# Window attention ahead of two feed-forward nets on one core: another layout for the global keys, their products by array quarters, and the attention outputs copied at another place

## The chip, the core and the metric

One NeuronCore of a Trainium2 chip runs the whole program. The metric is the device time of one execution in microseconds (us). The kernel before took 911.26 us (median of three runs, 911.12 to 912.29). In the text PE is TensorE, DVE is VectorE, ACT is ScalarE, POOL is GpSimd and SP is SyncE, as in the profile.

## The reference, cut to what matters

```python
# q_l, k_l, v_l: [4, 8, 512, 64]; q_g, k_g, v_g: [4, 8, 32, 64]
s_g   = scale * q_g @ concat(k_g, k_l)^T            # 32 global queries see all 544 keys
out_g = softmax(s_g) @ concat(v_g, v_l)
s_ll  = where(|i - j| <= 32, scale * q_l @ k_l^T, -1e9)   # local queries: a window ...
s_l   = concat(scale * q_l @ k_g^T, s_ll)                 # ... and the 32 global keys
out_l = softmax(s_l) @ concat(v_g, v_l)
x = concat(out_g, out_l)        # as [2176 tokens, 512]
h = x @ w_in;  x = (h * cos(h)) @ w_out              # first net, 512 -> 2048 -> 512
h = max(x @ w_in2, 0);  out = (h * h) @ w_out2       # second net, the same sizes
```

The four weight matrices come as float64. The chip makes float32 of their bits and splits each number into a high and a low part, so that a matrix product is three products of the parts.

## The kernel before, in words

**Items and steps.** The attention is cut into 40 items. For each batch and each pair of heads (there are 16 pairs, `p`) there are two `Local` items, each for 256 queries; behind each two pairs comes one `Global` item, so the items repeat as four Local and one Global. A loop over steps `s` runs them as a pipeline. In each step the list `CFG["order"]` gives the order in which parts are issued, and `CFG["lag"]` says of which item: the scores (`S`) of item s, the maxima and exponentials (`SM`) of item s, the reciprocals and the scaling (`RC`, `NM`) of item s-1, the transposes of the weights (`TM`) of item s-2, their evacuation (`TE`) of item s-3, the output products (`OM`) and the copy of the outputs (`OE`) of item s-4. Each engine works strictly in the order of issue, so the list also sets each engine's own order.

**A Local item.** `kT[p]` holds K^T of a pair of heads in eight blocks of 160 columns: 64 keys, the next 64 keys (a copy of the next block, made by POOL in `k_copy`), and the 32 global keys (also copied by POOL). The scores are eight products of a quarter of the PE array each (64 rows by 64 columns of it): rows by head, columns by half of the queries. DVE adds the mask and takes the maximum of each of four units, ACT makes the exponentials, POOL and DVE scale them, PE transposes them (`tw` for the window's part, `tg` for the global keys' part of all four units together), ACT brings them to SBUF, and `o_mm` multiplies by V. There the global keys' part is done with all 128 rows of the array: `VGZ` holds V of the global keys with zeros in the rows of the other units, and the product for each block of queries and each head uses one half of the array's columns. The outputs of an item go to one PSUM bank (6 and 7 by turns), and DVE copies them to `xt` with one instruction of 256 columns.

**Conversion of the weights.** `Feed` turns 64 pieces of the weights (a "job": 128 by 512 numbers) from float64 to float32 through five stages, one stage a step: a load, nothing, `conv_a` (POOL and ACT), `conv_b` (two DVE instructions, `CB` in the list), `conv_c` (POOL). `begin(rate)` starts a job when the credit is full. `split` makes the high part (two ACT instructions, L228) and on its next call the low part (one POOL and one DVE instruction, L214). Within the attention steps jobs start by a rate, `split` is called at the steps in `CFG["split"]`, and `CFG["sx"]` names the steps in which the first inputs of the nets are split (L744, L745).

**The nets.** From step 40 on `ffn_step` issues the products of the first net in between; 160 such steps follow, each with 12 products of 436 (or 512, 384) columns for `h` and 12 for `y`.

**PSUM banks.** Banks 0 and 1 take all transposes by turns, 2 the transposed global part, 3 to 5 the scores (two banks for an item, by turns), 6 and 7 the outputs.

The lines that the prediction touches: the scores L420, the maxima L436, the reciprocals L460 and L463, the scaling L475 (DVE for the first unit, POOL for three), the K copies L351, L353 and L361, the transposes L488 and L489, the output products L504 (global keys) and L516 (window), the copies of the outputs L529 and L633, the conversion L143, L146, L154, L155, L165, and the splits L228 and L214.

Of the kernel before, what the change touches and what calls it, by code (L numbers as in the profile page):

```python
# [19 lines left out]
P = 128  # L20
# [6 lines left out]
           'RC', 'NM', 'CB', 'LV', 'OE', 'TRQ', 'QE', 'KC', 'TM'],  # L27
# [19 lines left out]
 'free': -5,  # L47
 'kb': 'P',
 'split': [22, 24, 27, 29, 33],
 'sx': [32, 34, 37, 39],  # L50
 'arate': 0.5,
 'rate': 0.5,
 's0': 5,
# [6 lines left out]
RATE, ARATE, XD, NRING = CFG["rate"], CFG["arate"], CFG["xd"], CFG["nr"]  # L60

@with_exitstack
def kernel(
# [191 lines left out]

    KTB = 2 * 64 + SG
    masks = [ep.tile([P, 160], F32, name=f"mask{i}") for i in range(3)]
# [56 lines left out]
    def load_vg(b):  # L314
        for u in range(4):
            nc.sync.dma_start(
                VGZ[b % 2][32 * u : 32 * u + 32, :, u, :],
                v_g[b].rearrange("(k h) p d -> p k h d", h=2)[:, :, u // 2, :],
            )

    def tr_k(p):
        b, kk = divmod(p, NPAIR)
        tk = bank(BT, "tk")
        for c in range(4):
            nc.tensor.transpose(  # L325
                tk[:, c * P : (c + 1) * P],
                kn[p // 2][:, c, 2 * (p % 2) : 2 * (p % 2) + 2].rearrange("p h d -> p (h d)"),
                ident,
            )
        t = ep.tile([P, 8, KTB], F32, tag="kT", name="kT", bufs=3)  # L330
        kT[p] = t
        tks[p] = tk

    def k_evac(p):
        t, tk = kT[p], tks.pop(p)
        nc.scalar.activation(
            t[:, :, 0:64], tk.rearrange("p (j q) -> p j q", q=64), AF.Copy
        )
        if CFG["kb"] == "A":
            nc.scalar.activation(  # L340
                t[:, :, 128:KTB], tk[:, 0:SG].unsqueeze(1).to_broadcast([P, 8, SG]), AF.Copy
            )
        elif CFG["kb"] == "D":
            nc.vector.tensor_copy(
                t[:, :, 128:KTB], tk[:, 0:SG].unsqueeze(1).to_broadcast([P, 8, SG])
            )

    def k_copy(p):
        t = kT[p]
        one = dict(scalar1=1.0, scalar2=1.0, op0=ALU.mult, op1=ALU.mult)  # L350
        nc.gpsimd.tensor_scalar(t[:, 0:7, 64:128], t[:, 1:8, 0:64], **one)  # L351
        if CFG["kb"] == "P":
            nc.gpsimd.tensor_scalar(  # L353
                t[:, :, 128:KTB], t[:, 0, 0:SG].unsqueeze(1).to_broadcast([P, 8, SG]), **one
            )
        if p > 1:
            k_tail(p)

    def k_tail(p):
        b, kk = divmod(p, NPAIR)  # L360
        nc.gpsimd.tensor_scalar(  # L361
            kT[p][:, 7, 64:128], ktail[:, kk, b, :], 1.0, 1.0, op0=ALU.mult, op1=ALU.mult
        )
# [41 lines left out]

    class Local:
# [19 lines left out]

        def softmax(self):
            self.pt = lp.tile([P, 4, KTB], F32, tag="pt", name="pt", bufs=4)  # L430
            self.st = lp.tile([P, 3, 4], F32, tag="st", name="st", bufs=4)

            def unit(u):
                i = 2 * self.hb + u % 2
                m = masks[1] if i == 0 else masks[2] if i == 3 else masks[0]
                nc.vector.tensor_tensor_reduce(  # L436
                    out=self.pt[:, u, :],
                    in0=self.s[u // 2][:, 160 * (u % 2) : 160 * (u % 2) + 160],
                    in1=m,
                    scale=-0.125,  # L440
                    scalar=3.0e38,
                    op0=ALU.add,
                    op1=ALU.min,
                    accum_out=self.st[:, 0, u : u + 1],
                )
# [9 lines left out]
            return [lambda u=u: unit(u) for u in range(4)]  # L455
# [10 lines left out]
        def norm(self):  # L466
# [3 lines left out]
                self.pt[:, :, P:KTB],  # L470
                self.st[:, 2, :].unsqueeze(2).to_broadcast([P, 4, SG]),
                op=ALU.mult,
            )
            for u in range(4):
                (nc.vector if u < CFG["ndv"] else nc.gpsimd).tensor_scalar(  # L475
                    self.pt[:, u, 0:P],
                    self.pt[:, u, 0:P],
                    self.st[:, 2, u : u + 1],
                    1.0,
                    op0=ALU.mult,  # L480
                    op1=ALU.mult,
                )

        def t_mm(self):
            self.tw = bank(BT, "tw").rearrange("p (u q) -> p u q", u=4)
            self.tg = bank(BG, "tg")[:, 0:P]
            for u in range(4):
                nc.tensor.transpose(self.tw[:, u, :], self.pt[:, u, 0:P], ident)  # L488
# [11 lines left out]
        def o_mm(self):  # L500
            self.o = bank(BO, "o")[:, 0:256].rearrange("p (i q) -> p i q", i=2)
            for i in range(2):
                for h in range(2):
                    nc.tensor.matmul(  # L504
                        self.o[64 * h : 64 * h + 64, i, :],
                        lhsT=VGZ[self.b % 2][:, self.kk, 2 * h + i, :],
                        rhs=self.tgs,
# [3 lines left out]
                    )  # L511
                for half in range(2):
                    v = (VB if half else VA)[self.p // 2 % 2]
                    q = slice(64 * half, 64 * half + 64)
                    for h in range(2):
                        nc.tensor.matmul(  # L516
                            self.o[64 * h : 64 * h + 64, i, q],
                            lhsT=v[:, 2 * self.hb + i, 2 * (self.p % 2) + h, :],
                            rhs=self.tws[:, 2 * h + i, q],
# [5 lines left out]
        def o_evac(self):  # L525
            c0 = self.b * SL + 256 * self.hb
            dst, src = xt[:, self.kk, c0 : c0 + 256], self.o.rearrange("p i q -> p (i q)")
            if CFG["oe"][self.hb] == "D":
                nc.vector.tensor_copy(dst, src)  # L529
            else:  # L530
                nc.scalar.activation(dst, src, AF.Copy)


    class Global:
# [3 lines left out]
        def s_mm(self):  # L538
            self.s = []
            for n in (320, 256):  # L540
                s = bank(BT if CFG["sgb"] >> (n == 256) & 1 else BS, "sg")
                self.s.append(s)
                for i in range(2):
# [5 lines left out]
                        rhs=t[:, 0:5, 0:64] if n == 320 else t[:, 5:8:2, 0:128],  # L549
# [64 lines left out]
        def o_mm(self):  # L614
            self.o = bank(BO, "og")[:, 0 : 2 * SG].rearrange("p (i q) -> p i q", i=2)
# [33 lines left out]
    for h in range(2):  # L649
# [6 lines left out]
            out=masks[0][s, 64:128], in_=masks[0][s, 64:128], pattern=[[-1, 64]],  # L656
# [5 lines left out]
    nc.vector.memset(masks[2][64:128, 96:128], NEG)  # L662
# [361 lines left out]
```

## Time and profile before

| | |
|---|---|
| median of the runs | 911.26 us |
| the profiled execution's own time | 911.74 us |
| its span, first to last instruction | 910.0 us |
| busy PE / DVE / ACT / POOL | 890.7 / 502.5 / 439.4 / 447.8 us |
| products of the nets (L757 and L786), busy | about 403 us for h and 568 us for y, overlapping |
| attention steps 0 to 39, first scores to the first product of a net | 9.05 to 146.06 us |

The table's first lines say how long the program takes, the middle one how busy each engine was. A busy PE of 98% says little of its rate, since matmuls overlap; what tells is where PE stood still, and for that one looks at stretches. In a timeline the first number is the start, the second the time to the end of the last instruction of the row; the distance of two starts is what the engine needed, since neighbours overlap. Where a row ends in a bracket, the engine stood idle before it, and the bracket names who ended the wait. A group that works in its engine's own time and waits for nothing has no bracket; an instruction that sits on its engine until a semaphore comes can also show as a long duration.

### The profile page before, as it was taken

The page shows a single profiled execution, that of the slowest core. Times are in us where ns is not written, and L with a number is a line of the kernel's source. Part 1 is how long each engine was busy: PE and PEld are TensorE (multiplying, and loading weights), DVE is VectorE, ACT ScalarE, POOL GpSimd, SP SyncE. Part 2 cuts the span into 40 slices and gives each one's busy share as a digit, 9 for nine tenths or more (in the row PEclk, how much of TensorE's full clock was granted, in tenths as well). Part 3 has the DMA queues.
Part 4 walks back from the last instruction along what each step waited for, and adds up shares of the span by engine and source line. Part 5 has one row for each costly group of instructions (what it writes and reads, how often), then busy time and mean ns, then how long its engine had stood idle before and what let it go on. Part 6 is the DMA issues. An engine that isn't in the chain of part 4 may idle for free.

```text
span 910.0 us, 15436 instructions
## 1 busy us (share of the span) xinstructions
PE 890.7 (98%) x5720; PEld 793.7 (87%) x5720; DVE 502.5 (55%) x1058; ACT 439.4 (48%) x1036; POOL 447.8 (49%) x517
## 2 busy tenths in 40 slices
PE   7899999999999999999999999999999999999997
PEld 5777777999999999999999988889999888899996
DVE  5687899866776666765554483433422833232221
ACT  5778787665655545545444553333334632222211
POOL 4577888754574435744342484444423842222221
PEclk9999999999999999999999999999999999999999
DMA  7888643221122111121110021111100101010001
GB/s 168 192 192 195 165 129 94 71 70 53 49 62 70 47 53 61 50 70 47 47 47 1 1 70 47 53 44 66 47 1 1 47 1 47 1 47 1 35 35 36
DMA packets 82075, 57.10 MB, mean 63 GB/s; under 512 B 58320, under 2 KB 74704, under 8 KB 82000
## 3 DMA queue, kind: packets, MB, share of 16 engines
q1 hardware_dynamic: 79824, 55.59, 22.0%
q8 instruction: 45, 0.74, 0.3%
q10 hardware_dynamic: 2176, 0.52, 0.3%
q14 instruction: 30, 0.25, 0.1%
HBM read 47.45 MB, written 4.46 MB: 57 GB/s over the span
## 4 chain that ended last, share of the span: by engine, by line
PE 91%; DVE 3%; DMA 2%; ACT 1%; SPq 1%; POOL 1%; issue 1%; ACTq 0%; POOLq 0%; DVEq 0%
PE h L757 41%; PE y L786 41%; PE s L420 2%; PE tw L488 1%; PE o L504 1%; PE tq L368 1%; DVE pt L436 1%; PE o L516 1%; PE og L622 1%; DMA raw<-in_moe_w_out_dram 1%; PE sg L546 1%; PE tk L325 0%; ACT pt L446 0%; SPq L292 0%; PE twg L603 0%
## 5 line engine op out<-in xcount | busy, mean ns | idle before, releaser
L757 PE MATMUL h<-x,w 128*128 128x436 f32 (+3 forms) x1920 | 403.4, 358 | 0.0
L857 POOL TENSOR_TENSOR glo<-cr,ghi 128x436 fp32r<-128x436 f32 (+3 forms) x160 | 186.8, 1167 | 407.7 <-ACT ghi L851 393.9
L757 PEld LDWEIGHTS h<-x,w 128*128 128x128 f32 x1920 | 354.6, 188 | 27.5
L786 PE MATMUL y<-ghi,w 128*128 128x436 f32 (+1 forms) x640 | 177.6, 358 | 0.0
L846 DVE TENSOR_TENSOR cr<-h,cr 128x436 f32<-128x436 f32 (+3 forms) x160 | 96.6, 605 | 134.0 <-ACT cr L837 115.0
L786 PE MATMUL y<-w,ghi 128*128 128x512 f32 x544 | 168.4, 390 | 0.0
L745 DVE TENSOR_TENSOR x<-xt,x 128x436 fp32r<-128x436 f32 (+3 forms) x100 | 102.5, 1035 | 93.3 <-ACT x L744 78.3
L837 ACT ACTIVATE cr<-h 128x384 f32<-128x384 f32 (+1 forms) x80 | 42.8, 535 | 210.7 <-PE h L757 209.4
L786 PEld LDWEIGHTS y<-ghi,w 128*128 128x128 f32 x640 | 120.3, 188 | 6.1
L786 PEld LDWEIGHTS y<-w,ghi 128*128 128x128 f32 x544 | 101.4, 188 | 18.9
L786 PE MATMUL y<-glo,w 128*128 128x436 f32 (+1 forms) x320 | 114.8, 359 | 0.0
L786 PE MATMUL y<-w,glo 128*128 128x512 f32 x272 | 106.8, 393 | 0.0
L851 ACT ACTIVATE ghi<-cr 128x436 fp32r<-128x436 f32 (+3 forms) x160 | 89.7, 560 | 24.5 <-DVE cr L846 23.6
L831 ACT ACTIVATE ck<-h 128x436 int32<-128x436 f32 (+1 forms) x80 | 42.6, 532 | 113.1 <-PE h L757 113.1
L833 DVE SCALAR_TENSOR_TENSOR cr<-h,ck 128x436 f32<-128x436 f32 (+1 forms) x80 | 48.6, 607 | 84.9 <-ACT ck L831 84.9
L165 POOL TENSOR_TENSOR r<-cu,cc 128x512 uint32<-128x512 uint32 x64 | 85.0, 1328 | 2.0 <-DVE cc L155 2.0
L744 ACT ACTIVATE x<-xt 128x436 fp32r<-128x436 f32 (+3 forms) x100 | 55.1, 560 | 20.2 <-PE h L757 19.9
L786 PEld LDWEIGHTS y<-glo,w 128*128 128x128 f32 x320 | 60.1, 188 | 2.7
L786 PEld LDWEIGHTS y<-w,glo 128*128 128x128 f32 x272 | 51.0, 188 | 10.8
L842 ACT ACTIVATE cr<-cr,halfpi 128x436 f32<-128x436 f32 (+1 forms) x80 | 52.5, 657 | 10.1 <-DVE cr L833 10.1
L155 DVE SCALAR_TENSOR_TENSOR cc<-raw,cc 128x512 uint32<-128x512 uint32 x64 | 55.7, 870 | 0.0
L446 ACT ACTIVATE pt<-pt,st 128x160 f32<-128x160 f32 x128 | 53.3, 425 | 4.1 <-DVE st L436 4.1
(91 smaller groups left out, 907.4 us busy)
## 6 DMA issues: line engine op xcount, KB each, us to landing
raw<-in_moe_w_in_dram SPq DMA_DIRECT2D x32, 512.0 KB, 3.7
raw<-in_moe_w_out_dram SPq DMA_DIRECT2D x32, 512.0 KB, 3.5
vb<-va SPq DMA_DIRECT2D x16, 256.0 KB, 4.6
out_dram<-ypart SPq DMA_DIRECT2D x16, 256.0 KB, 2.1
qn<-in_q_l_dram SPq DMA_DIRECT2D x28, 128.0 KB, 3.7
va<-in_v_l_dram SPq DMA_DIRECT2D x24, 128.0 KB, 3.3
kn<-in_k_l_dram SPq DMA_DIRECT2D x21, 128.0 KB, 3.0
va<-in_v_l_dram SPq DMA_DIRECT2D x8, 96.0 KB, 3.2
```

The source lines that it names most:

```text
L155: lambda: v.scalar_tensor_tensor(c, t[:, :, 1].bitcast(U32), 0x80000000, c, op0=ALU.bitwise_and, op1=ALU.bitwise_or,),
L165: nc.gpsimd.tensor_tensor(ring[g][:, q, :].bitcast(U32), u, c, op=ALU.add)
L446: nc.scalar.activation(self.pt[:, u, :], self.pt[:, u, :], AF.Exp, bias=self.st[:, 0, u : u + 1], scale=-1.0, accum_out=self.st[:, 1, u : ...
L744: nc.scalar.activation(hi, xr, AF.Copy)
L745: return lambda: (nc.vector if kk in XD else nc.gpsimd).tensor_tensor(lo, xr, hi.bitcast(F32), op=ALU.subtract)
L757: nc.tensor.matmul(h, lhsT=w[:, ws, 0, kk * P : (kk + 1) * P], rhs=x, start=(k == 0), stop=(k == 3 * NK - 1),)
L786: nc.tensor.matmul(o, lhsT=l, rhs=r, start=(c_first and k == 0), stop=(c_last and k == 2))
L833: lambda: nc.vector.scalar_tensor_tensor(r, h, INV2PI, k, op0=ALU.mult, op1=ALU.subtract),
L842: nc.scalar.activation(ctmp[s], ctmp[s], AF.Sin, bias=halfpi, scale=TWOPI)
L846: nc.vector.tensor_tensor(r, hps.pop(s), r, op=ALU.mult)
L851: nc.scalar.activation(ghi[s], ctmp[s], AF.Copy)
L857: nc.gpsimd.tensor_tensor(lo, ctmp.pop(s), hi.bitcast(F32), op=ALU.subtract)
```

## The change

Five things are changed together.

1. **K^T's layout.** `kT[p]` is now nine blocks of 96 columns: 64 keys and then the 32 global keys. The 160 columns that a score product reads are the keys of a block, the global keys and the keys of the next block, in one run. POOL's copy of the next block (L351) is gone; the copy of the global keys (eight times) and of the tail remain. The masks move accordingly, and the scaled weights go to a new tile `pn`, since the window's two parts are now apart in `pt`.
2. **The global keys' output products by quarters.** The units are renumbered (u = 2 * block + head), so that the transposed global part holds a block of queries in each half of its rows. Each product takes 64 rows and 64 columns of the array, and the two blocks' outputs go to two banks. `out_half` gives each item a pair of 128-column pieces, one in bank 6 and one in bank 7, by turns left and right.
3. **The copy of the outputs** is two instructions of 128 columns, and `OE` stands right behind `SM` in the list, ahead of `RC`, `NM` and `CB`.
4. **The conversion** starts jobs at 13 named steps, and `split` is called at 21, 26, 31, 36 and 39.
5. In the nets' steps the rate of new jobs is 0.55 instead of 0.5.

```diff
-           'RC', 'NM', 'CB', 'LV', 'OE', 'TRQ', 'QE', 'KC', 'TM'],
+           'OE', 'RC', 'NM', 'CB', 'LV', 'TRQ', 'QE', 'KC', 'TM'],
- 'split': [22, 24, 27, 29, 33],
+ 'split': [21, 26, 31, 36, 39],
- 'arate': 0.5,
- 'rate': 0.5,
- 's0': 5,
+ 'begin': [9, 11, 14, 16, 19, 21, 24, 26, 29, 31, 34, 36, 39],
+ 'rate': 0.55,
...
+    obank = [ps.tile([P, 512], F32, tag=f"bank{k}", name="o") for k in BO]
+    def out_half():
+        k = turn["o"] = turn.get("o", 1) ^ 1
+        return [t[:, P * k : P * k + P] for t in obank]
...
-        t = ep.tile([P, 8, KTB], F32, tag="kT", name="kT", bufs=3)
+        t = ep.tile([P, 9, 64 + SG], F32, tag="kT", name="kT", bufs=3)
...
-        nc.gpsimd.tensor_scalar(t[:, 0:7, 64:128], t[:, 1:8, 0:64], **one)
...
+        nc.gpsimd.tensor_scalar(
+            t[:, 0:8, GK], t[:, 0, 0:SG].unsqueeze(1).to_broadcast([P, 8, SG]), **one
+        )
...
-                            rhs=kT[self.p][d, j, :],
+                            rhs=kT[self.p].rearrange("p j q -> p (j q)")[d, 96 * j : 96 * j + KTB],
...
-            self.pt = lp.tile([P, 4, KTB], F32, tag="pt", name="pt", bufs=4)
+            self.pt = lp.tile([P, 5, KTB], F32, tag="pt", name="pt", bufs=3)
...
-                    self.pt[:, u, 0:P],
-                    self.pt[:, u, 0:P],
+                    self.pn[:, u].rearrange("p (a q) -> p a q", a=2),
+                    windows(self.pt, u),
...
-            self.o = bank(BO, "o")[:, 0:256].rearrange("p (i q) -> p i q", i=2)
+            self.o = out_half()
             for i in range(2):
+                r = slice(64 * i, 64 * i + 64)
                 for h in range(2):
                     nc.tensor.matmul(
-                        self.o[64 * h : 64 * h + 64, i, :],
-                        lhsT=VGZ[self.b % 2][:, self.kk, 2 * h + i, :],
-                        rhs=self.tgs,
+                        self.o[i][64 * h : 64 * h + 64],
+                        lhsT=VGZ[self.b % 2][r, self.kk, 2 * i + h, :],
+                        rhs=self.tgs[r],
...
-            dst, src = xt[:, self.kk, c0 : c0 + 256], self.o.rearrange("p i q -> p (i q)")
...
+            for i in range(2):
+                nc.vector.tensor_copy(xt[:, self.kk, c0 + P * i : c0 + P * i + P], self.o[i])
...
-                cb = feed.begin(ARATE if due(CFG["free"]) is None else 0.0) if s >= CFG["s0"] else []
+                cb = feed.begin(1.0 if s in CFG["begin"] else 0.0)
```

PE's instructions of step 7 (the scores of item 7, then the output products of the Local item 3, then transposes), with the semaphores that a row waits for. Before:

```order
L420 MATMUL s<-kT,qT 64x160
L420 MATMUL s<-kT,qT 64x160 [waits DVE_49,PE_49]
L420 MATMUL s<-kT,qT 64x160 x6
L504 MATMUL o<-tgs,vgz_89 64x128 x2
L516 MATMUL o<-tws,va_85 64x64 x2
L516 MATMUL o<-tws,vb_87 64x64 x2
L504 MATMUL o<-tgs,vgz_89 64x128 x2
L516 MATMUL o<-tws,va_85 64x64 x2
L516 MATMUL o<-tws,vb_87 64x64 x2
```

The same place in the changed kernel:

```order
L423 MATMUL s<-kT,qT 64x160
L423 MATMUL s<-kT,qT 64x160 [waits DVE_49,PE_49]
L423 MATMUL s<-kT,qT 64x160 x6
L509 MATMUL o<-tgs,vgz_91 64x128 [waits DVE_49]
L509 MATMUL o<-tgs,vgz_91 64x128
L509 MATMUL o<-tgs,vgz_91 64x128 [waits DVE_49]
L509 MATMUL o<-tgs,vgz_91 64x128
L522 MATMUL o<-tws,va_87 64x64 x2
L522 MATMUL o<-tws,vb_89 64x64 x2
L522 MATMUL o<-tws,va_87 64x64 x2
L522 MATMUL o<-tws,vb_89 64x64 x2
```

The four products with the global keys now stand together, and the first for each bank waits for DVE. That wait is for the copies of the item just before: both items use the same two banks, in different columns.

DVE's instructions at the end of step 21 (the last maximum of item 21, then what follows it). Before:

```order
L436 ISA pt,st<-s,mask_84 128x160
L436 ISA st 128x1
L460 TENSOR_SCALAR st<-st 128x4
L463 RECIPROCAL st<-st 128x4
L475 TENSOR_SCALAR pt<-pt,st 128x128
L154 TENSOR_SCALAR cu<-cu 128x512
L155 SCALAR_TENSOR_TENSOR cc<-raw,cc 128x512
L529 COPY xt<-o 128x256
```

The same place in the changed kernel:

```order
L439 ISA pt,st<-s,mask_86 128x160
L439 ISA st 128x1
L534 COPY xt<-o 128x128 x2
L463 TENSOR_SCALAR st<-st 128x4
L466 RECIPROCAL st<-st 128x4
L479 TENSOR_SCALAR pn<-pt,st 128x128
```

The copy, now two, has moved ahead of the reciprocals; the conversion of this step (cu, cc) now stands one step later.

ACT's instructions from the exponentials of step 21 on (`tws`, `tls` and `tgs` are evacuations of transposes, `w` the high part of a weight tile). Before:

```order
L446 ACTIVATE pt,st<-pt,st 128x160 x4
L611 ACTIVATE tws<-twg 128x512
L612 ACTIVATE tls<-tlg 32x128
L336 ACTIVATE kT<-tk 128x8x64
L446 ACTIVATE pt,st<-pt,st 128x160 x4
L228 ACTIVATE w<-r 128x512 x2
L494 ACTIVATE tws<-tw 128x512
L498 ACTIVATE tgs<-tg 128x128
```

The same place in the changed kernel:

```order
L449 ACTIVATE pt,st<-pt,st 128x160 x4
L226 ACTIVATE w<-r 128x512 x2
L614 ACTIVATE tws<-twg 128x512
L615 ACTIVATE tls<-tlg 32x128
L343 ACTIVATE kT<-tk 128x8x64
L449 ACTIVATE pt,st<-pt,st 128x160 x4
L498 ACTIVATE tws<-tw 128x512
L502 ACTIVATE tgs<-tg 128x128
```

The two copies of the weight tile have moved one step forward, from behind the exponentials of step 22 to behind those of step 21.

## Rows read from the trace of the kernel before

**Rows 1.** Windows: stretch, its length, each engine's busy us (instructions), PE's clock, DMA.

```profile
59.50:75.17 15.67, 15.67 (x255) 12.75 (x254) 13.08 (x63) 12.62 (x50) 13.06 (x27) 1.00 0.92 200
75.17:93.41 18.24, 17.39 (x255) 13.75 (x254) 13.84 (x64) 14.25 (x53) 12.15 (x27) 0.91 0.80 188
...
126.42:146.30 19.88, 17.23 (x268) 13.04 (x268) 19.14 (x76) 16.47 (x60) 17.28 (x30) 1.00 0.36 108
...
161.40:900.00 738.60, 738.60 (x3628) 673.97 (x3627) 372.93 (x536) 319.76 (x609) 331.65 (x288) 1.00 0.13 41
```

**Rows 2.** Timeline of PE, step 17: start, us, line, shapes, records.

```profile
65.64 0.77 PE L420 MATMUL s<-kT,qT 64*64 64x160 f32 x16
66.35 0.44 PE L504 MATMUL o<-tgs,vgz 128*64 128x128 f32 x4
66.62 0.28 PE L516 MATMUL o<-tws,va 128*64 128x64 f32 x4
...
66.85 0.39 PE L504 MATMUL o<-tgs,vgz 128*64 128x128 f32 x4
67.07 0.28 PE L516 MATMUL o<-tws,va 128*64 128x64 f32 x4
67.18 0.29 PE L516 MATMUL o<-tws,vb 128*64 128x64 f32 x4
67.40 0.66 PE L325 MATMUL tk<-ident,kn 128*128 128x128 f32 x4
```

**Rows 3.** Timeline of PE, step 19, output products behind a Global item's scores.

```profile
73.03 0.39 PE L504 MATMUL o<-tgs,vgz 128*64 128x128 f32 x4
73.25 0.28 PE L516 MATMUL o<-tws,va 128*64 128x64 f32 x4
```

**Rows 4.** Timeline of PE, three rows in which PE had waited.

```profile
87.49 0.98 PE L368 MATMUL tq<-ident,qn 128*128 128x128 f32 x4 [0.61 <-ACT tws L494]
...
99.64 0.66 PE L603 MATMUL twg<-ident,ptg 128*128 128x128 f32 x4 [0.45 <-POOL ptg L595]
...
145.87 0.33 PE L488 MATMUL tw<-ident,pt 128*128 128x128 f32 x1 [0.37 <-POOL pt L475]
```

**Rows 5.** Windows: the stretch right behind the first of those waits.

```profile
87.67:91.09 3.42, 3.42 (x17) 2.31 (x18) 1.70 (x4) 2.78 (x11) 1.98 (x5) 0.50 0.81 170
```

**Rows 6.** Timeline of ACT, step 22, the weight tile's copies.

```profile
85.81 1.14 ACT L228 ACTIVATE w<-r 128x512 fp32r<-128x512 f32 x2
```

**Rows 7.** Timeline of POOL, 97 to 106 us.

```profile
97.62 1.26 POOL L165 TENSOR_TENSOR r<-cu,cc 128x512 uint32<-128x512 uint32 x1
...
100.57 1.07 POOL L475 TENSOR_SCALAR pt<-pt,st 128x128 f32<-128x128 f32 x3
...
103.20 2.18 POOL L475 TENSOR_SCALAR pt<-pt,st 128x128 f32<-128x128 f32 x3
105.36 0.56 POOL L351 TENSOR_SCALAR kT<-kT 128x448 f32<-128x448 f32 x1
```

**Rows 8.** Timeline of DVE, 118 to 131 us.

```profile
118.69 0.89 DVE L460 TENSOR_SCALAR st<-st 128x4 f32<-128x4 f32 x1
...
124.08 0.22 DVE L633 COPY xt<-og 128x64 f32<-128x64 f32 x1
...
127.96 0.62 DVE L154 TENSOR_SCALAR cu<-cu 128x512 uint32<-128x512 uint32 x1
128.51 0.68 DVE L155 SCALAR_TENSOR_TENSOR cc<-raw,cc 128x512 uint32<-128x512 uint32 x1
129.11 0.41 DVE L529 COPY xt<-o 128x256 f32<-128x256 f32 x1
129.44 0.71 DVE L745 TENSOR_TENSOR x<-xt,x 128x436 fp32r<-128x436 f32 x1
...
131.05 0.26 DVE L585 TENSOR_TENSOR stg<-stg 128x1 f32<-128x1 f32 x1
```

**Rows 9.** Timeline of PE, step 36, the first output product.

```profile
131.79 0.44 PE L504 MATMUL o<-tgs,vgz 128*64 128x128 f32 x4
```

More of the change, by code (lines that the diff above doesn't have):

```diff
@@ L59 @@
 GROUPS = CFG["groups"]
-RATE, ARATE, XD, NRING = CFG["rate"], CFG["arate"], CFG["xd"], CFG["nr"]
+RATE, XD, NRING = CFG["rate"], CFG["xd"], CFG["nr"]
 @with_exitstack
@@ L317, in load_vg @@
                 VGZ[b % 2][32 * u : 32 * u + 32, :, u, :],
-                v_g[b].rearrange("(k h) p d -> p k h d", h=2)[:, :, u // 2, :],
+                v_g[b].rearrange("(k h) p d -> p k h d", h=2)[:, :, u % 2, :],
             )
@@ L361, in k_tail @@
         nc.gpsimd.tensor_scalar(
-            kT[p][:, 7, 64:128], ktail[:, kk, b, :], 1.0, 1.0, op0=ALU.mult, op1=ALU.mult
+            kT[p][:, 8, 0:64], ktail[:, kk, b, :], 1.0, 1.0, op0=ALU.mult, op1=ALU.mult
         )
@@ L403, in load_qgn, with windows @@
         load_small(qgn, q_g[b], b)
+    def windows(t, u):
+        return t.rearrange("p u q -> p (u q)")[:, KTB * u : KTB * u + 192].rearrange(
+            "p (a q) -> p a q", a=2
+        )[:, :, 0:64]
     class Local:
@@ L437, in unit @@
                     out=self.pt[:, u, :],
-                    in0=self.s[u // 2][:, 160 * (u % 2) : 160 * (u % 2) + 160],
+                    in0=self.s[u % 2][:, 160 * (u // 2) : 160 * (u // 2) + 160],
                     in1=m,
@@ L453, in unit @@
                 )
-            return [lambda u=u: unit(u) for u in range(4)]
+            return [lambda u=u: unit(u) for u in (0, 2, 1, 3)]
         def recip(self):
@@ L469, in norm @@
                 self.pg,
-                self.pt[:, :, P:KTB],
+                self.pt[:, 0:4, GK],
                 self.st[:, 2, :].unsqueeze(2).to_broadcast([P, 4, SG]),
@@ L473, in norm @@
             )
+            self.pn = lp.tile([P, 4, P], F32, tag="pn", name="pn", bufs=2)
             for u in range(4):
                 (nc.vector if u < CFG["ndv"] else nc.gpsimd).tensor_scalar(
-                    self.pt[:, u, 0:P],
-                    self.pt[:, u, 0:P],
+                    self.pn[:, u].rearrange("p (a q) -> p a q", a=2),
+                    windows(self.pt, u),
                     self.st[:, 2, u : u + 1],
@@ L516, in o_mm @@
                         nc.tensor.matmul(
-                            self.o[64 * h : 64 * h + 64, i, q],
+                            self.o[i][64 * h : 64 * h + 64, q],
                             lhsT=v[:, 2 * self.hb + i, 2 * (self.p % 2) + h, :],
-                            rhs=self.tws[:, 2 * h + i, q],
+                            rhs=self.tws[:, 2 * i + h, q],
                             start=False,
@@ L526, in o_evac @@
             c0 = self.b * SL + 256 * self.hb
-            dst, src = xt[:, self.kk, c0 : c0 + 256], self.o.rearrange("p i q -> p (i q)")
[L528 to L531, printed above, removed]
+            for i in range(2):
+                nc.vector.tensor_copy(xt[:, self.kk, c0 + P * i : c0 + P * i + P], self.o[i])
     class Global:
@@ L548, in s_mm @@
                         lhsT=qgbd[:, kk, self.b, :],
-                        rhs=t[:, 0:5, 0:64] if n == 320 else t[:, 5:8:2, 0:128],
+                        rhs=t[:, 0:5, 0:64] if n == 320 else t[:, 5:9, 0:64],
                         start=True,
@@ L614, in o_mm @@
         def o_mm(self):
-            self.o = bank(BO, "og")[:, 0 : 2 * SG].rearrange("p (i q) -> p i q", i=2)
+            self.o = out_half()[0][:, 0 : 2 * SG].rearrange("p (i q) -> p i q", i=2)
             va = VA[(2 * self.b + self.g) % 2]
@@ L655 @@
         nc.gpsimd.affine_select(
-            out=masks[0][s, 64:128], in_=masks[0][s, 64:128], pattern=[[-1, 64]],
+            out=masks[0][s, 96:160], in_=masks[0][s, 96:160], pattern=[[-1, 64]],
             compare_op=ALU.is_ge, fill=NEG, base=0, channel_multiplier=1,
@@ L661 @@
     nc.vector.memset(masks[1][0:64, 0:32], NEG)
-    nc.vector.memset(masks[2][64:128, 96:128], NEG)
+    nc.vector.memset(masks[2][64:128, 128:160], NEG)
     nc.vector.memset(qgbd, 0.0)
```

20 lines of the change are left out of this document (4 added, 16 removed).

## Prediction

> **What bounds the kernel now.** I read the busy shares in slices first, then windows cut at the steps' first scores, then the timelines of PE, ACT, POOL and DVE inside the attention. In the stretch of the nets PE is busy for all of its 738.60 us [rows 1]: no edit here takes work from PE there, so the later start of conversion jobs and the rate of 0.55 count as nothing after 161 us. Their cover is PE's own stream; DVE, ACT and POOL are busy for half of it or less. What the change can move lies in the steps 0 to 43, before 161 us.
>
> There the limits differ. Steps 15 to 19 took 15.67 us and PE was busy for all of them [rows 1]: PE is the bound. Steps 20 to 24 took 18.24 us for the same kinds of items, so some 2.6 us of them are holes. From 126 to 146 us DVE is busy for 19.14 of 19.88 us: there DVE, with the exponentials that it waits for, is the bound, and PE's savings are worth nothing. The sum is made against the profiled execution's 911.74 us (span 910.0 and 1.74 around it), which stands 0.48 above the median of 911.26.
>
> **(a) Output products.** In step 17 four records of global products take 0.27 us from start to start the first time and 0.22 the second; four of window products take 0.11 in the middle and 0.22 before the transposes [rows 2]. So a pair of global products streams in 0.22, and a change of the array's shape costs 0.05 on entry and 0.11 on leaving, 0.16 in all. Behind a Global item's scores, which have the shape of the output products, the first group takes 0.22 without the 0.05 [rows 3]. Do four quarters run abreast? The scores' 16 records of 160 columns go out in 0.71 us with the change of shape in it [rows 2]; two abreast, at 0.22 for four records of 128 columns, they would need 1.10. So four quarters do, and the global products of an item fall from 0.44 to 0.22.
>
> Not every item gains that. There are 32 Local items. In 18 the scores just ahead have the quarters' shape, so no change of shape is added: -0.22 each. In 8 (steps 4, 9, ... 39) the scores are a Global item's, and two changes are added: -0.22 + 0.32 = +0.10. In 3 there are transposes of K's tail in between and in 3 no scores at all (steps 40 to 42): one change is added, -0.06 each. Over all 32: -3.5 us. But only up to step 31 is PE the bound, which leaves 14, 6 and 3 items: -2.7; and in steps 5 to 14 part of it is swallowed by waits for loads. I take **-2.4** (bounds: 0, if every wait just grows, and -3.5).
>
> **(b) The hole of step 23.** In step 22 ACT makes two copies of a weight tile, 1.14 us [rows 6], ahead of the evacuation that PE's next transposes need; PE stands still for 0.61 us [rows 4], and right behind that the granted clock is 0.50 for 3.42 us, that is 1.2 instead of 2.4 GHz [rows 5], which costs up to half of the stretch, 1.7. The split now comes in step 21. There the evacuation behind it is of the Global item's transposes, which PE needs a step later, and a bank that PE wants at the end of step 22: I count 0.3 of waiting. So -2.3 + 0.3 = **-2.0** (bounds: -2.3; and +1.7 if some other hole is followed by such a stretch and this one too).
>
> **(c) POOL.** The copy L351 is 0.56 us [rows 7], 16 times, 9.0 us less in all. POOL is not the bound on average, but some of PE's holes end with it: 0.45 at 99.64 and 0.37 at 145.87 [rows 4]. At 97.62 a conversion (1.26 us) stands ahead of the scaling that PE waits for [rows 7]. I take **-0.5** for the steps up to 31 (bounds 0 and -1.5).
>
> **(d) The copies on DVE.** 64 columns take 0.22 and 256 columns 0.41 [rows 8], so 128 take about 0.28 and two copies 0.57 instead of 0.41 by durations; from start to start the long one takes 0.33, and two short ones then 0.41. So +0.08 to +0.16 for an item, 2.6 to 5.1 us of DVE in all, hidden where PE is the bound. In steps 32 to 39 it is not hidden: 6 Local items' copies there make +0.5 to +1.0. Against it stands the new place: L460 at 118.69 took 0.89 us though it has four columns only: it sat on DVE until the exponentials were done [rows 8], and a copy ahead of it goes into that time. Each such wait gives back a copy's 0.4; I count two of them. And one more low part of a weight tile falls into these steps. Together **+0.6** (bounds -0.8 and +2.0). What the copies delay are the reciprocals, and through them POOL's scaling; transposes of an item come a step later, which covers it.
>
> **(e) The conversion.** By step 39 twelve jobs instead of ten have had their DVE part: two more of 1.15 us of DVE (0.55 and 0.60 from start to start [rows 8]) and their last stage of 1.26 on POOL [rows 7] in steps 10 to 39, and two fewer in steps 40 to 43. I take +0.5 for the former, most of it beside PE's work, and -0.8 for the latter, where PE waits as at 145.87 [rows 4]: **-0.3** (bounds -2.0 and +1.5). Conversion also slows POOL: its three scalings take 2.18 us beside it and 1.07 alone [rows 7], and the two are already inside the +0.5. The Trainium skill, "SBUF — State Buffer", section "Who interferes with whom", says that VectorE in a two-port mode and GpSimd lock each other out for a whole instruction. [...]
>
> The strided reads of `pt` and of `kT` keep their numbers of elements and I cost them at nothing; each 0.05 us in 32 DVE scalings would be 1.6 us of DVE.
>
> **Sum.** -2.4 - 2.0 - 0.5 + 0.6 - 0.3 = -4.6. From 911.74 that is 907.1, and on the scale of the median 906.7 us.
>
> **The new wait.** An item's first product in each bank now waits for DVE's copies of the item just before. In the order of before those copies stood at the end of a DVE step; now they follow the maxima. In the tight case of the trace, step 36, the maxima of step 35 ended where L585 starts, at 131.05, and the first output product started at 131.79 [rows 8, 9]: 0.74 us, of which two copies take 0.41 to 0.57, and PE comes up to 0.2 us sooner. So this wait is at the edge in DVE's worst steps and absent in the others. Queued behind it on PE are the window products, the transposes and the next scores, for which DVE waits in turn.
>
> **Rivals.**
> *Another engine is the bound nearly everywhere.* DVE gains 2.6 to 5.1 us of copies and 2.3 of conversion by step 39. If steps 15 to 31 run at DVE's pace, (a) is lost and (d) and (e) turn to about +2 together: 911.26 - 2.0 - 0.5 + 2 = 910.8. For it: 13.1 to 13.8 us of DVE in stretches of 15.7 and 18.2 [rows 1] with 1 to 2 conversions. Against it: in steps 15 to 19 PE never stopped.
>
> *The wait on the copies decides (slower).* Some 36 steps have output products behind such a wait. To turn -4.6 into +1.8 it needs 0.18 us in each on average; with 0.2 in each, 36 x 0.2 = 7.2, so 906.7 + 7.2 = 913.9. For it: the edge at step 36. Against it: DVE lags like that in few steps. The Trainium skill, "PSUM — Partial Sum Buffer", section "PSUM bank collisions raise a hardware error", says to guard PSUM by bank and quadrant and not by address. By that rule two halves of a bank are no two buffers, and the order of the changed kernel agrees: the wait is for the other half's copies.
>
> *Nearly all holes go.* With a full (a), (b) at -2.3, (c) at -1.5 and (e) at -2.0 the change is 911.26 - 9.3 = 902.0.
>
> *The quarters don't run abreast* for these products. Then (a) is anything from 0 to a loss of the 8 x 2 + 6 = 22 added changes of shape at 0.16, +3.5 us, instead of -2.4: 909.1 to 912.6, about 911. The scores speak against it [rows 2].
>
> **How the numbers follow.** Forecast 0.54, its own range 904.0 to 909.4. Another bound 0.18 (909.4 to 913.1, most of it within 0.2%). The wait on the copies 0.12. Nearly all holes gone 0.11. Quarters not abreast 0.05. A run of this kernel can be told from no change beyond about 0.2%, 1.8 us. Faster by more: 0.54 + 0.11 and a little of the others, 0.67; within: 0.20; slower: 0.13. The range of 902.5 to 912.3 leaves out some 0.06 below and 0.11 above.
>
> **What would show it.** Right: output products of a Local item behind Local scores 0.22 us shorter; two more changes of shape behind a Global item's scores; no half clock near 88 us; steps 15 to 31 shorter by 0.5 us in five, and more in 20 to 24; L351 gone; DVE in the last stretch as busy as before. Wrong: output products that wait for DVE's copies in most steps, a half clock at another place, or five steps that take DVE's time rather than PE's.

## The result and the profile after

The changed kernel took 921.88 us (median of four runs, 920.11 to 923.37); the kernel before, beside it on the same chip, 911.77 (911.12 to 913.22). The ratio is 1.0106, with a 95% interval of 1.0086 to 1.0125. It is slower by 10 us where I forecast 4.6 faster, and outside my range. The profiled execution took 921.91 us, its span 920.0.

How late the steps start against before, by the first scores of each step:

| first scores of step | 6 | 8 | 19 | 20 | 24 | 26 | 28 | 30 | 39 | end of the span |
|---|---|---|---|---|---|---|---|---|---|---|
| after minus before, us | -1.0 | +3.2 | +3.6 | +5.6 | +4.0 | +3.0 | +3.5 | +6.5 | +8.9 | +10.0 |

So the time is lost in four places: steps 6 and 7, step 19, step 29, and the steps 30 to 38. Steps 23 to 25 win. The last 1.3 us are lost in the nets; whether the change has a part in that is open (last section).

Windows of the changed kernel, same columns as [rows 1]; the stretches are steps 15 to 19, 20 to 24, 34 to 38, and the nets:

```profile
62.76:80.79 18.03, 15.63 (x254) 11.84 (x254) 14.94 (x67) 13.42 (x53) 12.76 (x26) 1.00 0.93 204
80.79:96.67 15.88, 15.16 (x255) 11.91 (x254) 14.98 (x67) 13.82 (x52) 12.36 (x24) 1.00 0.78 183
130.55:148.56 18.01, 15.70 (x243) 10.93 (x242) 17.52 (x74) 14.11 (x54) 14.90 (x25) 1.00 0.39 117
165.86:915.00 749.14, 749.14 (x3701) 681.77 (x3700) 387.96 (x538) 321.12 (x611) 335.13 (x290) 1.00 0.12 40
```

Steps 15 to 19, where PE never stopped before, now hold 2.4 us of holes. Steps 20 to 24 are 2.4 us shorter, at full clock (1.00 instead of 0.91), though PE's own holes there are nearly as long as before (0.72 us, 0.85 before). PE is still busy throughout the nets. The output products did get shorter. Timeline of PE in the changed kernel, step 17, as [rows 2]:

```profile
69.34 0.77 PE L423 MATMUL s<-kT,qT 64*64 64x160 f32 x16
69.94 0.40 PE L509 MATMUL o<-tgs,vgz 64*64 64x128 f32 x8
70.27 0.34 PE L522 MATMUL o<-tws,va 128*64 128x64 f32 x4
...
70.67 0.29 PE L522 MATMUL o<-tws,vb 128*64 128x64 f32 x4
70.88 0.66 PE L332 MATMUL tk<-ident,kn 128*128 128x128 f32 x4
```

From the scores to the next transposes it is 1.54 us instead of 1.76: the 0.22 that I forecast, and the quarters do run abreast.

Now the loss of step 29, the clearest one. Timeline of the changed kernel, rows of SP, ACT, POOL and PE in order of time:

```profile
99.68 2.05 SPq L323 DMA_DIRECT2D vgz<-in_v_g_dram  x4
101.77 1.36 SPq L316 DMA_DIRECT2D vb<-va  x1
103.17 0.60 SPq L317 DMA_DIRECT2D vb<-va  x1
103.86 3.07 SPq L299 DMA_DIRECT2D qn<-in_q_l_dram  x4
107.10 0.38 SPq L129 DMA_DIRECT2D raw<-in_moe_w_out_dram  x1
...
113.24 0.66 ACT L144 ACTIVATE cc<-raw 128x512 uint32<-128x512 uint32 x1 [4.39 <-DMA raw<-in_moe_w_out_dram]
113.81 0.41 ACT L449 ACTIVATE pt<-pt,st 128x160 f32<-128x160 f32 x1
...
113.30 0.65 POOL L141 TENSOR_SCALAR cu<-raw 128x512 f32<-128x512 f32 x1 [3.82 <-DMA raw<-in_moe_w_out_dram]
...
116.08 1.11 PE L492 MATMUL tw<-ident,pn 128*128 128x128 f32 x4 [3.13 <-ACT tws L498]
```

A conversion job that starts in step 26 (from 100.05 us) issues its raw load behind V's second layout and Q, at 107.10. The data are there at 113.2. Two steps after the start, ACT's and POOL's part of the job stands in their queues ahead of the exponentials and the scaling, and both engines wait for about 4 us. PE gets its wait of 3.13 us from that, and half the clock behind it:

```profile
30.63:37.45 6.82, 5.71 (x67) 4.41 (x69) 1.85 (x10) 3.30 (x13) 1.45 (x4) 0.50 0.76 185
115.96:119.37 3.41, 3.29 (x35) 2.49 (x37) 2.40 (x9) 2.50 (x10) 3.41 (x9) 0.50 0.82 211
```

These windows are the two stretches at a granted clock of 0.50 (1.2 instead of 2.4 GHz); the one of before [rows 5] is gone. The first stands behind a wait in step 6, for the load of K's last 32 rows:

```profile
31.74 0.60 PE L377 MATMUL ttail<-ident,ktn 32*128 32x32 f32 x4 [3.73 <-DMA ktn<-in_k_l_dram]
```

Who waited for the raw data between 40 and 135 us (us, times) in the changed kernel:

```profile
  ACT cc L144: 10.2, 4
  POOL cu L141: 6.9, 3
```

Before, ACT's part waited 2.2 us for it, once. That was the job of step 11, whose load stands behind V's second layout and Q in both kernels. The changed kernel adds two jobs in such a place, those of steps 16 and 26, and the two holes in steps 19 and 29 stand behind these two. The job of step 16, on ACT and POOL:

```profile
76.98 0.70 ACT L144 ACTIVATE cc<-raw 128x512 uint32<-128x512 uint32 x1 [2.53 <-DMA raw<-in_moe_w_out_dram]
77.04 0.68 POOL L141 TENSOR_SCALAR cu<-raw 128x512 f32<-128x512 f32 x1 [2.11 <-DMA raw<-in_moe_w_out_dram]
```

### The profile page after: what moved, and what is told of

Its sections match the earlier page's. It is cut to its first block, busy times and chain, and to the rows that moved or that the text cites. A ratio compares the mean times of both kernels' runs of the same rounds, so it can differ in the third digit from the quotient of the medians.

```text
span 920.0 us, 15463 instructions
## 1 busy us (share of the span) xinstructions
PE 891.9 (97%) x5720; PEld 788.1 (86%) x5720; DVE 516.4 (56%) x1090; ACT 440.1 (48%) x1036; POOL 441.6 (48%) x501
## 3 DMA queue, kind: packets, MB, share of 16 engines
q1 hardware_dynamic: 79824, 55.59, 21.6%
## 4 chain that ended last, share of the span: by engine, by line
PE 89%; DVE 5%; ACT 2%; DMA 2%; POOL 1%; SPq 1%; issue 0%; ACTq 0%; POOLq 0%; DVEq 0%
PE h L760 41%; PE y L789 41%; DVE pt L439 2%; PE s L423 2%; PE tw L492 1%; ACT pt L449 1%; PE o L625 1%; PE o L522 1%; DMA raw<-in_moe_w_out_dram 1%; PE sg L549 1%; DVE xt L534 1%; PE tq L365 0%; PE tk L332 0%; PE o L509 0%; DVE pn L479 0%
## 5 line engine op out<-in xcount | busy, mean ns | idle before, releaser
L854 ACT ACTIVATE ghi<-cr 128x436 fp32r<-128x436 f32 (+3 forms) x160 | 89.7, 560 | 20.9 <-DVE cr L849 20.0
L153 DVE SCALAR_TENSOR_TENSOR cc<-raw,cc 128x512 uint32<-128x512 uint32 x64 | 62.2, 971 | 0.0
L152 DVE TENSOR_SCALAR cu<-cu 128x512 uint32<-128x512 uint32 x64 | 53.2, 832 | 12.0 <-POOL cu L141 12.0
```

What stands on the lines that cost most here:

```text
L152: lambda: v.tensor_scalar(u, u, 3, None, op0=ALU.logical_shift_left),
L153: lambda: v.scalar_tensor_tensor(c, t[:, :, 1].bitcast(U32), 0x80000000, c, op0=ALU.bitwise_and, op1=ALU.bitwise_or,),
L854: nc.scalar.activation(ghi[s], ctmp[s], AF.Copy)
```

## The experiments

"Changed" is the changed kernel. Ratios are to the kernel before, run beside each.

| run | us | ratio, interval |
|---|---|---|
| x1 changed, old conversion | 913.17 | 1.0002 [0.9989, 1.0015] |
| x2 before, new conversion | 921.22 | 1.0072 [1.0044, 1.0099] |
| x3 changed, raw loads one step sooner | 913.30 | 1.0009 [0.9997, 1.0020] |
| x4 changed, K's tail loaded sooner | 922.17 | 1.0092 [1.0066, 1.0118] |
| x5 quarters and layout alone | 920.23 | 1.0097 [1.0066, 1.0127] |
| x6 copies' place alone | 913.75 | 1.0018 [1.0001, 1.0034] |
| x7 x3 with other splits | 914.46 | 1.0016 [0.9998, 1.0034] |
| x8 before, new conversion, raw sooner | 912.15 | 0.9995 [0.9980, 1.0010] |
| x9 changed, ACT's part behind the exponentials | 923.99 | 1.0125 [1.0104, 1.0146] |
| x10 changed, light conversion | 908.19 | 0.9955 [0.9938, 0.9971] |
| x11 x10 and K's tail sooner | 908.46 | 0.9953 [0.9935, 0.9972] |
| x12 before, light conversion | 907.47 | 0.9948 [0.9931, 0.9965] |
| x13 changed, raw load first in its step | 919.20 | 1.0087 [1.0056, 1.0118] |
| x14 changed, conversion's work a step later | 917.06 | 1.0053 [1.0034, 1.0072] |

Each run's profiled execution in five stretches, us, cut at the first scores of a step; y is the first product of `y`, from which the nets count. These are single executions, so the medians above need not agree with their sums.

| | to step 8 | 8 to 29 | 30 to 38 | 39 to y | nets |
|---|---|---|---|---|---|
| before | 35.7 | 75.1 | 28.9 | 21.5 | 748.7 |
| x2 | 36.2 | 80.3 | 31.2 | 21.7 | 750.1 |
| x8 | 35.5 | 71.4 | 30.5 | 21.6 | 748.7 |
| x12 | 37.3 | 70.4 | 29.8 | 20.4 | 749.7 |
| changed | 38.9 | 78.4 | 31.2 | 21.4 | 750.1 |
| x1 | 38.3 | 72.8 | 29.2 | 21.8 | 750.1 |
| x3 | 36.9 | 70.7 | 31.4 | 21.6 | 750.1 |
| x4 | 36.7 | 78.3 | 32.1 | 23.1 | 750.1 |
| x5 | 35.3 | 76.4 | 32.6 | 21.6 | 750.1 |
| x7 | 38.1 | 73.9 | 29.7 | 21.4 | 750.1 |
| x10 | 35.7 | 69.6 | 29.6 | 20.9 | 751.0 |
| x14 | 38.4 | 72.5 | 32.5 | 22.9 | 750.1 |

**Which part costs: x1 and x2.** The conversion is exchanged between the two kernels.

```
x1 (changed): 'split': [22, 24, 27, 29, 33], rate 0.5
 - cb = feed.begin(1.0 if s in CFG["begin"] else 0.0)
 + cb = feed.begin(ARATE if due(CFG["free"]) is None else 0.0) if s >= CFG["s0"] else []
x2 (before): the reverse, with the 13 steps and the splits of the changed kernel
```

> The changed kernel with the conversion schedule of before (jobs begun at rate 0.5 from step 5, weight tiles split in steps 22, 24, 27, 29 and 33, rate 0.5 in the nets). Theory 1 (the 13 conversion steps cost the time, because their loads stand on SP behind the loads of an array's rows and the conversion's copy then holds the exponentials on ACT): 913 to 916 us, steps 18 and 28 lose their waits of about 2 and 3.8 us and the hole of step 23 comes back with 2.3. Theory 2 (the copies of the outputs behind the maxima, by wait or by DVE time, cost it): 920 to 923 us. Under both the step 6 keeps its half clock.

> The kernel before with only the new conversion schedule (13 named steps, splits in 21, 26, 31, 36 and 39, rate 0.55 in the nets). Theory 1: slower by 3 to 7 us, 915 to 919, with ACT's conversion copy waiting for the raw load in steps 13, 18 and 28. Theory 2: 909 to 912, since the hole of step 23 goes and nothing else is lost.

x1 came out as theory 1 says, and x2 2 us above its range (by the ratio, 6.6 us above before): the loss goes with the conversion's schedule, and comes with it to the kernel before. In x2, too, ACT and POOL wait for the raw data:

```profile
  ACT cc L146: 10.7, 3
  POOL cu L143: 9.1, 3
```

**Is it the late load: x3 and x8.**

```
-                    conv_load(*job)
+                    job in raw or conv_load(*job)
...
+ (at BG) if s + 1 in CFG["begin"]: conv_load(*feed.jobs[0])
```

> The changed kernel with each raw load of the 13 conversion steps issued one step sooner, the conversion itself where it was. Theory 1 (late raw loads): 914 to 917 us, ACT's copy waits for the raw load for under 2 us in all instead of 9.3. Theory 2 (copies behind the maxima): 920 to 923 us. A third possibility, that the conversion's own work on ACT, POOL and DVE costs the time wherever its data come from: also 920 to 923, but with ACT's waits for the raw load gone.

> The kernel before with the new conversion schedule and its raw loads one step sooner. Theory 1 (the late raw loads are all that costs): 912 to 914, like x3 and 8 us below x2. If x3 is level with before only because the quarters pay for what the conversion still costs: 915 to 917, 2 to 4 us above x3.

In both kernels the loads' lead of one step gives back 7 to 9 us (by the ratios 0.97% from the changed kernel to x3 and 0.77% from x2 to x8). Within each pair the conversion work is the same, so it is the late load that costs. In x3 nothing on ACT or POOL waits for the raw data between 40 and 135 us. The same job as above, in x3, is loaded in time, and its ACT part has no bracket:

```profile
92.69 0.35 SPq L129 DMA_DIRECT2D raw<-in_moe_w_out_dram  x1
...
102.98 0.67 ACT L144 ACTIVATE cc<-raw 128x512 uint32<-128x512 uint32 x1
```

x8 is level with x3 within their intervals, which says a second thing: the quarters and the copies are not what pays the loss back.

**By which path: x9, x14, x13.**

```
x9:  (in conv_a) - nc.scalar.activation(c, ...)   + feed.cc = lambda: nc.scalar.activation(c, ...)
     (behind i.softmax()) + feed.stage[2] and feed.cc()
x14: - self.stage = [None] * 5 ... a, b, c = self.stage[2:]
     + self.stage = [None] * 6 ... a, b, c = self.stage[3:]
x13: + (first in the step) s in CFG["begin"] and conv_load(*feed.jobs[0])
```

> The changed kernel with one edit: in the attention ACT's conversion copy stands behind the step's exponentials instead of ahead of them; the raw loads stay as late as they are. Theory 1 (the loss comes because the copy, waiting for a late load, holds the exponentials on ACT): 914 to 917 us, 5 to 8 below the changed kernel, and no exponentials that start after such a wait. Rival (late loads cost because the whole conversion comes late, or because the loads disturb others): 920 to 923.

> The changed kernel with one edit: in its own step the raw load is issued first on SP, ahead of the loads of V's second layout and of Q, in the six steps that have them; all else stays. If the place behind those six DMAs (some 5 us of issue by the timeline of SP) is what makes the loads late: 913 to 916 us, as x3. If the load needs a whole step's lead, as x3 gave it: 918 to 921.

> The changed kernel with its raw loads where they are on SP and every stage of the conversion's work (ACT, POOL, DVE) one step later. If the loss comes because the work on ACT and POOL stands in their queues and waits for a late load, whichever of the two it holds: 912 to 916 us, as x3. If the loss comes from where the raw loads stand among the other loads (they delay K, V and Q): 920 to 923, as the changed kernel.

x9 refuted theory 1 in its narrow form. Taking ACT's part out of the exponentials' way saved nothing. Timeline of x9, ACT, POOL and then PE:

```profile
112.34 0.66 ACT L144 ACTIVATE cc<-raw 128x512 uint32<-128x512 uint32 x1 [2.49 <-DMA raw<-in_moe_w_out_dram]
...
112.46 0.64 POOL L141 TENSOR_SCALAR cu<-raw 128x512 f32<-128x512 f32 x1 [3.63 <-DMA raw<-in_moe_w_out_dram]
...
114.86 1.50 POOL L479 TENSOR_SCALAR pn<-pt,st 128x128 f32<-128x128 f32 x3
...
115.71 1.18 PE L492 MATMUL tw<-ident,pn 128*128 128x128 f32 x3 [1.85 <-POOL pn L479]
```

POOL holds its scaling behind the same load, and ACT now waits for it ahead of the next evacuation instead. The load has two waiters, on two in-order engines, and PE is now stopped by way of POOL; that ACT's path alone would stop it too was not tried. x14, which moves both, falls to 917: less than expected. ACT's part still waits 4.4 us there, in three places. In the profiles x14 is longer than x3 by 1.8 us in steps 8 to 29, where those waits are, by 2.4 us from step 30 to y, and by 1.5 us before step 8; what causes the last two is not shown. In x13 ACT's waits for raw fall to 0.9 us; its profile is the fastest of its four executions (915.88 us). But what the load was put ahead of now comes late, K's tail for one:

```profile
63.73 0.40 PE L377 MATMUL ttail<-ident,ktn 32*128 32x32 f32 x4 [1.63 <-DMA ktn<-in_k_l_dram]
```

By the ratios the first place in its own step gives back 0.2%, which is not clear of noise, and the lead of a whole step 0.97%. The DMA engines are busy for 0.78 to 0.93 of steps 15 to 24 in the changed kernel, a raw load takes 3.5 to 6.1 us from issue to landing between 40 and 135 us, and even the first place in its step was not early enough for all.

**The other parts: x5 and x6.**

```
x5 (changed, old conversion): 'OE' back behind 'LV' in CFG["order"]
x6 (before): 'OE' moved up behind 'SM', one copy of 256 columns as before
```

> The quarters, the two output banks and K^T's new layout alone: conversion as before, and the outputs' copies at the end of a DVE step as before. If the saving on TensorE (0.22 us in 18 steps) counts and the copies behind the maxima took it back in x1: 2 to 4 us below before, about 909. If the saving is swallowed by waits for loads in the first 15 steps and by DVE in the last ten, wherever the copies stand: within 1 us of before and of x1, about 912 to 913. If the quarters themselves cost something (a wait between halves of a bank, short copies): above x1, 914 or more.

> The kernel before with its outputs' copies right behind the maxima and nothing else. If the place of the copies costs time (they stand ahead of the reciprocals and the conversion on DVE): 1 to 3 us above before. If it is neutral: within 1 us. If it frees the output bank sooner and fills DVE's waits for the exponentials, as my prediction counted: 0.5 to 1 us below.

x5 is the wait that I priced as a rival, in the kernel where it does exist. What PE waited for, 40 to 160 us (us, times, longest), in x5:

```profile
PE o L509 <- DVE xt L534: 4.7, 5, 1.4
...
PE o L625 <- DVE xt L534: 1.6, 3, 0.7
```

and in x1, where the copies stand behind the maxima:

```profile
PE o L625 <- DVE xt L534: 0.3, 1, 0.3
```

With halves of two banks, an item's products wait for the copies of the item just before; late copies cost 7 to 9 us (920.2 against 913.2 in x1; by the ratios 0.95%; in the profiles 7.0 us in steps 8 to 38), and their new place takes this away. On the kernel before, which has no such wait, the new place gains nothing (x6). In one place DVE comes later to the copies of Q^T, and PE waits for those:

```profile
63.94 0.43 PE L380 MATMUL ttail<-ident,ktn 32*128 32x32 f32 x4 [0.78 <-DVE qT L374]
```

**The wait of step 6: x4 and x11; the splits: x7.**

```
x4:  - if s in (4, 14, 24):  + if s in (2, 12, 22):   (load_ktn)
x11: the same in x10
x7 (x3): 'split': [22, 24, 27, 29, 39]
```

> The changed kernel with the load of the last 32 rows of K (for the next batch) issued two steps sooner, after step 2, 12 and 22 instead of 4, 14 and 24. Theory 3 (PE waits 3.73 us for this load in step 6 and the clock falls to half for 6.8 us behind it): 917 to 919 us, the step 6 takes about 3 us less, and no half clock near 31 us. If the wait only moves to the next load in the queue or the clock falls for another reason: 920 to 923 us.

> x10 with the load of the last 32 rows of K two steps sooner, as in x4. If the half clock behind PE's wait for that load (2 to 3 us in steps 6 and 7 of x1, x3 and x7) is a loss of its own: 1 to 3 us below x10. If the early steps are set by all the loads together, and this wait only moves: within 1 us of x10.

> The changed kernel with raw loads one step sooner as in x3, and with the weight tiles split in steps 22, 24 and 27 (halves finished by 29) instead of 21, 26 and 31 (by 36). Theory: in x3 the splits of steps 21 and 26 stand on ACT ahead of the Global item's evacuations (PE waits 0.35 and 0.93 us) and those of 31 and 36 add one ACT split and one DVE half to the last stretch, which DVE bounds (30 to 39 took 2.3 us longer than in x1). Moved, 2 to 3.5 us below x3: about 910, 2 us below before. Rival (the last stretch is long because of the conversion jobs, not the splits): as x3, 913.

Theory 3 falls. In x4 step 6 takes 2.76 us instead of 7.98, but PE waits for Q in step 3 (1.59 us). The half clock has only moved too: from 20.20 to 27.03 us the granted clock is 0.50. Step 8 starts 2.2 us sooner, and the time stays all the same: what was won early is gone by y. x11 is level with x10, but says little, since x10's own profile has no such wait in step 6 (2.76 us there too). So what sets the early steps is not shown.

x7 was no better than x3, but its theory came true in half. Steps 30 to 38 took 29.7 us instead of 31.4, close to the 29.2 of x1, although step 31 alone was longer (3.95 us instead of 2.49). So it is mostly the splits of steps 31 and 36 that cost there, not the jobs. The gain was lost again in steps 8 to 29, 73.9 us instead of 70.7: with the split back in step 22, steps 23 and 24 take 9.33 us instead of 7.09.

**A faster version: x10 and x12.** Eight jobs are enough for the first four weight tiles of the nets. So no job starts between steps 27 and 38.

```
- 'split': [21, 26, 31, 36, 39],  'begin': [..., 26, 29, 31, 34, 36, 39],  'rate': 0.55,
+ 'split': [24, 29, 34, 39],      'begin': [..., 26, 39],                  'rate': 0.6,
```

> The changed kernel with raw loads one step sooner as in x3, no conversion job begun between step 27 and 38 (eight jobs done by step 30, the rest in the nets at rate 0.6), splits in steps 24, 29 and 34. Theory (what x3 loses in steps 30 to 39 is DVE's and ACT's work for conversion and splits; steps 30 to 39 take 31.5 us there and 29.2 in x1): steps 30 to 39 in 28 to 29 us, 2 to 3 us below x3, that is 910 to 911.5, about 1 to 2 below before. If the work is missing later and PE waits in the nets for a weight tile: 914 or more.

> The kernel before with the conversion of x10 (raw loads one step sooner, no job begun between step 27 and 38, splits in 24, 29 and 34, rate 0.6 in the nets). Against x10 it leaves out the quarters, the two output banks, K^T's layout and the copies behind the maxima. If these are worth nothing net: within 1 us of x10. If they are worth what is left of my term (a): 1 to 3 us above x10. If they cost: 1 to 2 us below x10, and then this is the fastest version, 909 to 910.

Both beat both kernels, by 4 to 5 us against before, and their intervals exclude 1. Windows from step 27 to the last attention outputs, x8 and then x12:

```profile
96.38:154.97 58.59, 54.24 (x764) 42.37 (x764) 51.70 (x186) 48.62 (x163) 49.54 (x81) 1.00 0.49 124
```

```profile
98.18:153.79 55.61, 52.56 (x764) 42.35 (x764) 42.81 (x178) 45.58 (x157) 39.53 (x74) 1.00 0.38 93
```

3.0 us less, with 8.9 us less on DVE and 10 on POOL; from x3 to x10 it is 59.46 to 55.78. And x12 without the quarters is as fast as x10 with them in the times. The profiles qualify this: up to y x10 is 2.2 us ahead of x12, 1.6 of it before step 8 and 0.8 in steps 8 to 29, and its nets then take 1.2 us longer.

## Why the prediction was wrong

**The step that failed is (e).** I took -0.3 for the moved conversion, with bounds of -2.0 and +1.5, by adding the DVE and POOL time of two jobs. It measured +8: in the profiles up to y +8.2 from before to x2 and +7.9 from x1 to the changed kernel, by the ratios +6.6 us (interval 4.0 to 9.0) and some +9.5. I priced the instructions of a job and not its load. The 13 steps put six jobs into steps in which SP has other DMAs to issue first, ten of them in the case shown. Before, four of the jobs that the rate started stood so (steps 11, 21, 31 and 36); the two new ones are those of steps 16 and 26. Conversion work that finds no data blocks two in-order engines, and +5.2 to +5.6 us of the loss lie in steps 8 to 29, where this happens. My list of what counts in a moved step had DVE and POOL only. The trace of before had a sign of it, a wait of 2.2 us of ACT for raw data behind the same loads, which the sum left out. Moreover, the -0.8 for steps 40 to 43 did not come: from the outputs of step 39 to those of step 43 it took 16.45 us before and 16.35 in x3. And in steps 30 to 38 the new conversion costs 1.6 to 2.3 us besides (31.45 us in x3 to 29.18 in x1, 30.53 in x8 to 28.89 before), by x7 mostly for its splits. DVE was the bound there, as (d) said; I had given that stretch one more low part, and of the copies of a split on ACT nothing.

The Trainium skill, "DMA: Bandwidth & Descriptors", section "Rules for kernel authors", says to issue a DMA early and wait for it late. x3 and x8 agree, with 7 to 9 us.

**(a) was right in mechanism and too large.** Each clean step is 0.22 us shorter, a step behind a Global item's scores 0.10 longer, both as forecast. But between steps 8 and 30, x10 takes 69.58 us and x12 70.38, with POOL's missing copy in it: -0.8, where my own counts give -1.8 for these steps. Seven steps show the full 0.22 (-1.54), two the half (-0.22), five the +0.10 (+0.50), and three (16, 21 and 26) got no shorter but longer (+0.49 together); I had counted ten full ones here, and 14 up to step 31. In the times it can't be told: x1 against before, x3 against x8 and x10 against x12 lie within one another's intervals, which are wider than 0.8 us. The Trainium skill, "TensorEngine Tiling (Array Packing)", section "Tiling Modes", says that a change of the tiling mode drains the array; the +0.10 behind a Global item's scores agrees, and over a quarter of the gain went there.

**(b) was right in size, in part by luck:** steps 23 and 24 took 7.09 us instead of 9.30 (-2.2 for my -2.0). But what is large there is the half clock, and it does not come with every such split. x1, x5, x6 and x7 keep the split in step 22 and take 7.24, 7.75, 7.63 and 9.33 us. x5, x6 and x7 have the wait behind it (0.59, 0.57 and 0.59 us), but only x7 has a granted clock of 0.50 behind that, as before had; x1 has neither. So the split explains the wait and not that the clock falls, and the 2.6 us that I called holes in steps 20 to 24 were 0.85 us of idle PE and, for the rest, mostly that half clock. The new splits made holes of their own in steps 22 and 27 (0.35 us, for my 0.3, and 0.93 us behind ACT's evacuation).

**(c) and (d) hold roughly in their busy times.** POOL's busy time fell by 6.2 us without L351 [rows 7], for my 9.0; what (c) gave in time no run shows apart from (a). One reading of [rows 7] was off: not a conversion alone slowed the three scalings by 1.11 us. The first took 1.06 us beside the conversion's second instruction and the second the usual 0.37. The third took 0.80, beside the low part of a weight tile on DVE:

```profile
104.35 0.79 DVE L214 TENSOR_TENSOR w<-r,w 128x512 fp32r<-128x512 f32 x1
```

The copies' durations in the changed kernel (ns, least, median, most):

```profile
L534 DVE COPY xt<-o x64: 274/282/293, 22.6 to 164.4; 128x128 f32<-128x128 f32 x64
```

That is the 0.28 that I had estimated between the lengths of [rows 8]. With the old conversion (x1) steps 30 to 38 take 0.3 us more than before, where (d) had +0.6; with the light one (x10 against x12) they take 0.25 us less.

**The new wait and the rivals.** The wait on the copies does not show in the changed kernel; its price, which I had put at 7.2 us, is about what x5 lost, though the size is luck: I had spread it over 36 steps, and in x5 PE waits in eight places between 40 and 160 us. So the mechanism was real, and the move of the copies had already met it; what made the kernel slower came from elsewhere. The quarters run abreast, so that rival is out. "A half clock at another place" was on my list of signs that I was wrong, and there were two.

Open is the early part: where PE first waits for loads (Q in step 3 or K's tail in step 6) differs from one profile to the next with the same program up to there (x1 and x10, for one, or before and x12), so a difference of 1 to 3 us before step 8 is not charged to any edit here. That goes for the 3.2 us of the changed kernel too. Nor is the half clock there a mark of the change: eleven of the sixteen profiles have such a stretch between 20 and 40 us, x2 and x12 among them. Nor was it tried to take the conversion's work out of the way of both engines altogether, with the loads left late.

## What to carry to other kernels

A step that is moved takes its load along: look up where that load then stands in the issuing queue and how long it takes to land, and count every engine on which its consumer stands ahead of critical work; here moving one of two consumers saved nothing (x9). Work that isn't needed until later can be taken out of the stretch that another engine bounds: that was worth more here than all savings on TensorE. And a saving per instruction counts only in steps in which its engine, not a load or another engine, ends last.

## What was not expected of the hardware

The nets ran at two rates, in kernels whose products in the nets are the same. Groups of PE between 165 and 225 us, with the mean ns of one product, before and then after:

```profile
L757 PE MATMUL h<-x,w 128*128 128x436 f32 x138 | 28.6, 355 | 0.0
```

```profile
L760 PE MATMUL h<-x,w 128*128 128x436 f32 x152 | 32.4, 360 | 0.0
```

In before, x8 and x12 twelve products take 2.32 us until some 73 us into the nets and 2.37 after that; in all others they take 2.37 nearly from the start. That makes 1.3 us; the granted clock is shown as 1.00 in all of them, and why is open. All eleven profiles of kernels with the quarters have the slower rate, and so have x2 and x6, which lack them; so it needs no quarters, but that the change has no part in it is not shown. Executions of before spread over 909.4 to 916.0 us beside x1, more than the interval of its first three runs let expect.
